# Softcap attention and a bilinear layer on one core: the reciprocals' DMAs from GpSimd, the raw weights requested earlier

## The chip, the cores and the metric

One core of a Trainium2 chip runs the whole program. The metric is the device time of one launch in microseconds (us), lower is better. The engines are TensorE (PE), VectorE (DVE), ScalarE (ACT), GpSimd (POOL) and SyncE (SP). Each works through its own queue of instructions in a fixed order; a DMA is an instruction in the queue of the engine that issues it.

## What is computed

```python
scores = q @ k.T / sqrt(64)                   # 4 batches, 12 heads, 448 tokens, head size 64
scores = 30 * tanh(scores / 30)
attn   = exp(scores - max) / (sum(exp(scores - max)) + 1e-09)
x      = attn @ v                             # joined over heads: 1792 tokens x 768
out    = ((x @ w_a) * (x @ w_b)) @ w_out      # 768 -> 1536 -> 768
```

The inputs q, k, v are fp32, the three weights fp64 (two 32-bit words for each number).

## The kernel before

**Attention.** The 48 heads are taken as 24 pairs, `pi` = 0 to 23; pairs 0 to 11 are batches 0 and 1 (group 0), the others group 1. For a pair, `load_pair` issues nine loads (ldk, ldq, ldv) on SyncE; `prep_pair` transposes k and q on VectorE (tk, tq); `scores` makes psc on TensorE, tanh and exp on ScalarE (L224, L225), and the sum of the probabilities over the key chunks on VectorE (L229, L232, L233). One step later `attend` multiplies by v (pv) and `normalize` ends the pair: 16 small matmuls give the sums of the denominators, VectorE takes the reciprocal `rec` (L268), and because the reciprocals lie along the wrong axis they go through DRAM: `rd[pi]` is written (L269), then read back twice, each time spread over 64 partitions of `den` (L273, two transfers). VectorE multiplies pv by den (L274). For group 0 VectorE rounds the product to `xhi` (L283) and GpSimd makes the rest `xlo` (L284); for group 1 the product is stored in DRAM and read back later. In group 1 pv holds one of the two PSUM buffers of psc until L274.

**The bilinear layer.** `ffn(g)` runs over 12 slices `f` of the hidden size: products with w_a and w_b in three passes of split fp32 (L377 to L379), their product split again, and after every third slice the products with w_out (L408 to L410). It is a generator whose matmuls are laid between the steps of the attention of the next group; what is left of group 0 and all of group 1 comes at the end.

**The weights.** The units are a, b, o of each slice, 36 in all, in the order of use. `load64` requests a raw fp64 unit of 768 KB on SyncE into one of two buffers. `ready_w` makes fp32 of it: two ScalarE passes (L337, L338), three on VectorE (L339 to L341; L341 is the last to read the raw buffer), one addition on GpSimd (L342), and a store `wd` for group 1's use on SyncE (L343). `split_w` makes the high and low part (L359, L360; the low part of a and b on GpSimd) and calls `ready_w` for units up to four ahead. `ready_w` is called first after the steps of `pi` = 8 and begins by requesting raw units up to the one after its own.

**What sets the order.** The steps of a pair follow the letters of `order` (P prep, A attend, S and T scores, N normalize, F a stretch of the layer). That is only the order of the program text: when the kernel is built, a planner simulates the engines with its own cost estimates and writes each engine's queue, an instruction going in when the planner believes its inputs ready, and text order deciding between those that are ready. `tc.keep_in_program_order` pins the first five raw loads behind the instruction of SyncE that stands before them in the text.

Of the kernel before, what the change touches and what calls it, by code (L numbers as in the profile page):

```python
# [117 lines left out]
def kernel(  # L118
# [11 lines left out]
    nc = tc.nc  # L130
    B, H, S, D = q.shape
    NT, DM = out.shape
    DFF = w_a.shape[1]
    P = 128
# [11 lines left out]
    NPG = NPAIR // NG  # L146
    NW = 3 * NF
# [3 lines left out]
    Q = 32  # L151
    AHEAD = 4
# [6 lines left out]
    rd = [dr.tile([2 * NCH, CP], F32, tag=f"rd{i}", name=f"rd{i}") for i in range(NPAIR)]  # L159
# [17 lines left out]
    def f32(ap):  # L177
        return ap.bitcast(F32)
# [10 lines left out]
    raw, stk, prob, pvs = {}, {}, {}, {}  # L189
# [60 lines left out]
    def normalize(pi):  # L250
        del raw["v", pi], stk[pi]
        g, r = divmod(pi, NPG)
        bh, hp = divmod(r, NP)
        t, ts = pvs.pop(pi)
        if ts is None:
            ts = ps_1.tile([P, 512], F32, tag="ps1", name=f"sum_{pi}")
        for m in range(2):
            for i in range(4):
                j, c = divmod(2 * i + m, NCH)
                nc.tensor.matmul(  # L260
                    ts[i * Q : (i + 1) * Q, :CP],
                    sel[:, m],
                    psum[pi % 2][:, j, c * CP : (c + 1) * CP],
                    start=(m == 0),
                    stop=(m == 1),
                )
        rec = sm.tile([P, CP], F32, tag="rec", name=f"rec_{pi}")
        nc.vector.reciprocal(rec, ts[:, :CP])  # L268
        nc.sync.dma_start(rd[pi], rec[0 : P : Q // 2])  # L269
        den = sm.tile([P, S], F32, tag="den", name=f"den_{pi}")  # L270
        for j, o in enumerate(own):
            row = rd[pi][j * NCH : (j + 1) * NCH].rearrange("(o c) p -> o (c p)", o=1)
            nc.sync.dma_start(den[o], row.to_broadcast([D, S]))  # L273
        nc.vector.tensor_mul(den, t[:, :S], den)  # L274
        if g == 0:
            split_x(r, den, nc.gpsimd)
        else:
            nc.sync.dma_start(xd[r], den)

    def split_x(r, xt, eng):  # L280
        bh, hp = divmod(r, NP)
        cs = slice(bh * S, (bh + 1) * S)
        nc.vector.tensor_copy(xhi[:, hp, cs], xt)  # L283
        eng.tensor_sub(xlo[:, hp, cs], xt, f32(xhi[:, hp, cs]))  # L284
# [13 lines left out]
    pos = {"raw": 0, "conv": 0, "split": 0}  # L298

    def load64():  # L300
        t = pos["raw"]
        if t >= NW:
            return
        pos["raw"] += 1
        nm, f, _ = seq[t]
        cs = slice(f * P, (f + 1) * P)
        w = {"a": w_a, "b": w_b, "o": w_out}[nm].bitcast(I32)
        rt = wp.tile([P, DM, 2], I32, tag="w64", name=f"w64{nm}_{f}", bufs=2)
        if nm == "o":
            ld64 = nc.sync.dma_start(rt.rearrange("p n t -> p (n t)"), w[cs, :])  # L310
        else:
            ld64 = nc.sync.dma_start(
                rt.rearrange("p (k f) t -> p k (f t)", k=NK),
                w.rearrange("(k p) f -> p k f", p=P)[:, :, 2 * f * P : 2 * (f + 1) * P],
            )
        if t < AHEAD + 1:
            tc.keep_in_program_order(ld64)
        wraw[t] = rt

    def ready_w():  # L320
        t = pos["conv"]
        if t >= len(seq):
            return
        pos["conv"] += 1
        nm, f, g = seq[t]
        if g:
            wt = wp.tile([P, DM], F32, tag="wt", name=f"wr{nm}_{f}", bufs=AHEAD)
            nc.sync.dma_start(wt, wd[nm, f])
            wfull[t] = wt
            return  # L330
        while pos["raw"] < min(t + 2, NW):
            load64()
        rt = wraw.pop(t)
        hw, lw = rt[:, :, 1], rt[:, :, 0]
        lr = wp.tile([P, DM], I32, tag="wr", name=f"wl{nm}_{f}", bufs=1)
        wt = wp.tile([P, DM], I32, tag="wt", name=f"wt{nm}_{f}", bufs=AHEAD)
        nc.scalar.activation(lr, lw.bitcast(U32), AF.Copy, scale=2.0**-29)  # L337
        nc.scalar.activation(f32(wt), f32(hw), AF.Abs)  # L338
        nc.vector.tensor_scalar_max(f32(wt), f32(wt), TINY_HI)  # L339
        nc.vector.tensor_scalar(wt, wt, 3, 0x3FFFFFFF, op0=ALU.logical_shift_left, op1=ALU.bitwise_and)  # L340
        nc.vector.scalar_tensor_tensor(wt, hw, -0x40000000, wt, op0=ALU.bitwise_and, op1=ALU.bitwise_or)  # L341
        nc.gpsimd.tensor_tensor(wt, wt, lr, op=ALU.add)  # L342
        nc.sync.dma_start(wd[nm, f], f32(wt))  # L343
        wfull[t] = f32(wt)

    def split_w():
        t = pos["split"]
        if t >= len(seq):
            return
        pos["split"] += 1  # L350
        nm, f, g = seq[t]
        wt = wfull.pop(t)
        tag, bufs = ("o", GF) if nm == "o" else ("ab", 3)
        hi = wp.tile([P, DM], F32R, tag=f"wh{tag}", name=f"wh{nm}_{g}_{f}", bufs=bufs)
        lo = wp.tile([P, DM], F32R, tag=f"wl{tag}", name=f"wl{nm}_{g}_{f}", bufs=bufs)
        if g and nm == "b":
            nc.vector.tensor_copy(hi, wt)
        else:
            nc.scalar.copy(hi, wt)  # L359
        (nc.vector if nm == "o" else nc.gpsimd).tensor_sub(lo, wt, f32(hi))  # L360
        wspl[nm, g, f] = (hi, lo)
        while pos["conv"] < min(t + AHEAD, len(seq)):
            ready_w()
# [57 lines left out]
    with ExitStack():  # L421
        load_pair(0)
        nc.sync.dma_start(capt[:, 3:4], cap.rearrange("(a b) -> a b", b=1).to_broadcast([P, 1]))
        make_identity(nc, ident)
        load_pair(1)
        nc.vector.memset(sel, 0.0)
        for m in range(2):
            nc.vector.memset(sel[:, m, m * Q // 2 : (m + 1) * Q // 2], 1.0)
        nc.vector.tensor_scalar_mul(capt[:, 4:5], capt[:, 3:4], -1.0)
        nc.vector.tensor_max(capt[:, 5:6], capt[:, 3:4], capt[:, 4:5])  # L430
        nc.vector.tensor_scalar(bounded, capt[:, 5:6], CAP_MAX, None, op0=ALU.is_le)
        nc.vector.tensor_scalar_min(capt[:, 0:1], capt[:, 5:6], CAP_MAX)
        nc.vector.reciprocal(capt[:, 6:7], capt[:, 0:1])
        nc.vector.tensor_scalar_mul(capt[:, 1:2], capt[:, 6:7], 1.0 / math.sqrt(D))
        nc.scalar.activation(capt[:, 7:8], capt[:, 0:1], AF.Exp, scale=-1.0)
        nc.vector.tensor_scalar_mul(capt[:, 2:3], capt[:, 7:8], 1e-9 / R)

        gen, done, p0 = None, 0.0, 0
        total = NF * 72 * S + NTI * 2 * NF * 3 * HALF

        def run_ffn(upto):
            nonlocal gen, done
            while gen is not None and done < upto:
                try:
                    done += next(gen)
                except StopIteration:
                    gen = None

        prep_pair(0)
        for pi in range(NPAIR + 1):  # L450
            order = "PASNFTF" if pi <= NPG else "SFANPFTF"
            slices = 0
            for step in order:
                if step == "P" and pi + 1 < NPAIR:
                    prep_pair(pi + 1)
                elif step == "A" and pi > 0:
                    attend(pi - 1)
                elif step == "N" and pi > 0:
                    normalize(pi - 1)
                elif step == "S" and pi < NPAIR:  # L460
                    scores(pi, 0)
                    if pi + 2 < NPG - 1:
                        load_pair(pi + 2)
                elif step == "T" and pi < NPAIR:
                    scores(pi, 1)
                elif step == "F":
                    slices += 1
                    run_ffn(total * (pi - p0 + slices / order.count("F")) / (NPG + STRETCH))
            if NPG - AHEAD <= pi < NPG:
                ready_w()  # L470
            if pi == NPG - 1:
                for _ in range(3):
                    split_w()
            if NPG - 1 <= pi + 2 < NPAIR:
                load_pair(pi + 2)
            if pi and pi % NPG == 0:
                run_ffn(1e18)
                gen, done, p0 = ffn(pi // NPG - 1), 0.0, pi + 1
        run_ffn(1e18)
# [37 lines left out]
```

## Time and profile before

| | us |
|---|---|
| median of 3 runs (782.0 to 782.84) | 782.74 |
| the profiled execution | 784.88 |
| its span, first to last instruction | 783.1 |
| TensorE busy | 732.6 (94%) |
| VectorE, ScalarE, GpSimd busy | 424.1, 331.6, 185.4 |
| mean granted clock of TensorE | 0.978 |

The profiled execution is 2.1 us longer than the median, and 1.8 us of it lie outside its span. "Busy" of TensorE counts a matmul that waits inside its pipeline as well. DMA-issuing instructions do not count as busy on any engine; they show as SPq (SyncE's queue) in the timeline. All DMAs of the program stand in SyncE's queue.

### The profile page before, as it was taken

The numbers are of one execution on the slowest core, as the hardware profiler recorded it, in microseconds if no ns is written. First come the engines' busy times: TensorE is split into PE (matmuls) and PEld (weight loads), VectorE is DVE, ScalarE is ACT, GpSimd is POOL, SyncE is SP. The second block draws the span as 40 slices with busy tenths as digits, with TensorE's granted clock in tenths as the row PEclk, the third lists the DMA queues.
The fourth block names the chain that finished last, engine by engine and source line by source line (L and its number), as shares of the span: only waits on it lengthen the run. The fifth ranks groups of instructions, "written<-read, shape, count | busy, mean of one in ns | idle before, by whom it ended". The sixth has DMA issues, their size and how long they took to land.

```text
span 783.1 us, 10042 instructions
## 1 busy us (share of the span) xinstructions
PE 732.6 (94%) x3888; PEld 560.7 (72%) x3888; DVE 424.1 (54%) x562; ACT 331.6 (42%) x402; POOL 185.4 (24%) x102
## 2 busy tenths in 40 slices
PE   5699776997899999998999999999999999999996
PEld 1233223675587677775777787999999999999996
DVE  4576789898624876465665654733213342243222
ACT  5588587575655755354651631022232202212110
POOL 0011244364302343025340221002102201200100
PEclk9899989999899999999899999999999999999999
DMA  6455687885643664336442133542102102111002
GB/s 122 92 105 114 164 180 203 243 228 185 192 120 120 184 198 136 96 108 195 143 156 85 41 105 109 184 135 81 41 21 100 41 21 81 62 41 41 1 35 111
DMA packets 151926, 90.47 MB, mean 116 GB/s; under 512 B 114624, under 2 KB 139456, under 8 KB 151872
## 3 DMA queue, kind: packets, MB, share of 16 engines
q1 hardware_dynamic: 151872, 89.77, 40.3%
q8 instruction: 32, 0.52, 0.3%
q14 instruction: 22, 0.18, 0.1%
HBM read 67.24 MB, written 22.50 MB: 115 GB/s over the span
## 4 chain that ended last, share of the span: by engine, by line
PE 61%; DMA 17%; DVE 11%; issue 4%; SPq 3%; ACT 3%; POOL 1%; DVEq 0%; ACTq 0%; POOLq 0%
PE po L408 6%; PE po L410 6%; PE po L409 6%; PE phb L377 6%; PE phb L378 6%; PE phb L379 6%; PE pha L377 6%; PE pha L379 6%; PE pha L378 6%; DMA den<-rd 5%; PE psc L223 4%; DMA rd<-rec 4%; PE pv L245 2%; DMA xl<-xd 2%; DMA w64o<-in_moe_w_out_dram 2%
## 5 line engine op out<-in xcount | busy, mean ns | idle before, releaser
L223 PE MATMUL psc<-tq,tk 64*128 64x448 f32 (+1 forms) x384 | 97.1, 602 | 25.9 <-DVE den L274 12.3
L408 PE MATMUL po<-who,gh 128*128 128x384 f32 x336 | 114.1, 340 | 1.0 <-DVE acc L414 0.8
L409 PE MATMUL po<-wlo,gh 128*128 128x384 f32 x336 | 112.5, 335 | 0.0
L410 PE MATMUL po<-who,gl 128*128 128x384 f32 x336 | 112.5, 335 | 0.0
L377 PE MATMUL phb<-xhi,whb 128*128 128x448 f32 x288 | 108.0, 375 | 0.0
L377 PE MATMUL pha<-xhi,wha 128*128 128x448 f32 x288 | 107.6, 374 | 0.0
L378 PE MATMUL phb<-xlo,whb 128*128 128x448 f32 x288 | 106.9, 371 | 0.0
L379 PE MATMUL phb<-xhi,wlb 128*128 128x448 f32 x288 | 106.6, 370 | 0.0
L379 PE MATMUL pha<-xhi,wla 128*128 128x448 f32 x288 | 106.2, 369 | 0.0
L378 PE MATMUL pha<-xlo,wha 128*128 128x448 f32 x288 | 106.1, 369 | 0.0
L224 ACT ACTIVATE pf<-psc,capt 128x896 f32<-128x896 f32 x96 | 85.1, 909 | 44.3 <-PE psc L223 43.6
L223 PEld LDWEIGHTS psc<-tq,tk 64*128 64x128 f32 (+1 forms) x384 | 29.5, 180 | 68.6 <-issue 35.4
L225 ACT ACTIVATE pf<-pf,capt 128x1792 f32<-128x1792 f32 (+1 forms) x48 | 77.0, 1604 | 1.2
L414 DVE TENSOR_TENSOR acc<-po,acc 128x384 f32<-128x384 f32 x84 | 45.9, 554 | 48.2 <-PE po L410 48.1
L408 PEld LDWEIGHTS po<-who,gh 128*128 128x128 f32 x336 | 63.0, 188 | 8.5 <-issue 3.2
L384 DVE TENSOR_TENSOR asb<-phb,asb 128x448 f32<-128x448 f32 x48 | 29.8, 621 | 68.7 <-PE phb L379 68.6
L245 PE MATMUL pv<-pf,ldv 128*64 128x448 f32 x288 | 63.6, 563 | 2.5 <-ACT pf L225 2.5
L409 PEld LDWEIGHTS po<-wlo,gh 128*128 128x128 f32 x336 | 63.1, 188 | 0.8 <-issue 0.7
L410 PEld LDWEIGHTS po<-who,gl 128*128 128x128 f32 x336 | 63.0, 188 | 0.7 <-issue 0.7
L377 PEld LDWEIGHTS phb<-xhi,whb 128*128 128x128 f32 x288 | 55.0, 191 | 11.9 <-issue 6.1
L377 PEld LDWEIGHTS pha<-xhi,wha 128*128 128x128 f32 x288 | 54.5, 189 | 11.7 <-issue 6.1
L386 DVE TENSOR_TENSOR gl<-asb,gh 128x448 fp32r<-128x448 f32 x48 | 51.0, 1063 | 21.6 <-ACT gh L385 21.4
(73 smaller groups left out, 971.0 us busy)
## 6 DMA issues: line engine op xcount, KB each, us to landing
w64a<-in_moe_w_a_dram SPq DMA_DIRECT2D x12, 768.0 KB
w64b<-in_moe_w_b_dram SPq DMA_DIRECT2D x12, 768.0 KB
w64o<-in_moe_w_out_dram SPq DMA_DIRECT2D x12, 768.0 KB
ldk<-in_k_dram SPq DMA_DIRECT2D x96, 56.0 KB
ldq<-in_q_dram SPq DMA_DIRECT2D x96, 56.0 KB
ldv<-in_v_dram SPq DMA_DIRECT2D x24, 224.0 KB
den<-rd SPq DMA_DIRECT2D x48, 112.0 KB
out_dram<-acc SPq DMA_DIRECT2D x13, 384.0 KB
```

Of the source, the lines that this page charges most:

```text
L223: nc.tensor.matmul(to, tk[o, at : at + (P if n == 2 else R)], tq[o], start=True, stop=True)
L224: nc.scalar.activation(pf[:, 2 * i : 2 * i + n], psc[:, :n, :S], AF.Tanh, scale=capt[:, 1:2])
L225: nc.scalar.activation(pf, pf, AF.Exp, scale=capt[:, 0:1])
L245: nc.tensor.matmul(t[j * D : (j + 1) * D, :S], tv[:, j * (NC3 + 1) + c], p, start=(c == 0), stop=False)
L377: nc.tensor.matmul(t[:, :S], wh[:, kk], xhi[:, kk, cs], start=(kk == 0), stop=False)
L378: nc.tensor.matmul(t[:, :S], wh[:, kk], xlo[:, kk, cs], start=False, stop=False)
L379: nc.tensor.matmul(t[:, :S], wl[:, kk], xhi[:, kk, cs], start=False, stop=(kk == NK - 1))
L386: nc.vector.tensor_sub(gl[:, cs], asb[h], f32(gh[:, cs]))
L408: nc.tensor.matmul(t[:, :HALF], gh[:, cs], wh, start=(f == fs[0]), stop=False)
L409: nc.tensor.matmul(t[:, :HALF], gh[:, cs], wl, start=False, stop=False)
L410: nc.tensor.matmul(t[:, :HALF], gl[:, cs], wh, start=False, stop=(f == fs[-1]))
L414: nc.vector.tensor_add(acc[:, ti, hs], t[:, :HALF], acc[:, ti, hs])
```

## The change

The write of `rd` and the two reads into `den` are issued by GpSimd instead of SyncE. The first two raw weight units are requested after the steps of `pi` = 6 instead of inside the first `ready_w` (after `pi` = 8), and each `ready_w` requests the unit two ahead at its own end, behind its store, instead of leaving it to the start of the next `ready_w`. Buffers stay as they are: two raw ones.

```diff
         rec = sm.tile([P, CP], F32, tag="rec", name=f"rec_{pi}")
         nc.vector.reciprocal(rec, ts[:, :CP])
-        nc.sync.dma_start(rd[pi], rec[0 : P : Q // 2])
+        nc.gpsimd.dma_start(rd[pi], rec[0 : P : Q // 2])
         den = sm.tile([P, S], F32, tag="den", name=f"den_{pi}")
         for j, o in enumerate(own):
             row = rd[pi][j * NCH : (j + 1) * NCH].rearrange("(o c) p -> o (c p)", o=1)
-            nc.sync.dma_start(den[o], row.to_broadcast([D, S]))
+            nc.gpsimd.dma_start(den[o], row.to_broadcast([D, S]))
...
-        while pos["raw"] < min(t + 2, NW):
+        while pos["raw"] < min(t + 1, NW):
             load64()
...
         nc.sync.dma_start(wd[nm, f], f32(wt))
         wfull[t] = f32(wt)
+        while pos["raw"] < min(t + 3, NW):
+            load64()
...
+            if pi == NPG - AHEAD - 2:
+                for _ in range(2):
+                    load64()
             if NPG - AHEAD <= pi < NPG:
                 ready_w()
```

## Rows read from the trace of the kernel before

**Rows 1.** The page's first lines: span, and busy time of each engine.

```profile
span 783.1 us, 10042 instructions
PE 732.6 (94%) x3888; PEld 560.7 (72%) x3888; DVE 424.1 (54%) x562; ACT 331.6 (42%) x402; POOL 185.4 (24%) x102
```

**Rows 2.** Busy time of each engine in stretches of 20 us, 100 to 160.

```profile
100.00:120.00 20.00, 16.02 (x72) 4.20 (x68) 18.72 (x20) 14.82 (x17) 11.56 (x6) 0.83 0.77 182
120.00:140.00 20.00, 15.09 (x88) 7.60 (x88) 19.27 (x25) 16.51 (x17) 8.44 (x5) 0.91 0.79 217
140.00:160.00 20.00, 19.58 (x107) 14.19 (x107) 17.39 (x20) 11.04 (x15) 10.10 (x6) 1.00 0.80 242
```

**Rows 3.** Timeline of one pair's loop, 45 to 58, and the sixth reciprocal later.

```profile
45.63 0.85 DVE L268 RECIPROCAL rec<-sum 128x112 f32<-128x112 f32 x1
48.23 1.10 SPq L273 DMA_DIRECT2D den<-rd  x2
50.03 1.79 ACT L225 ACTIVATE pf<-pf,capt 128x1792 f32<-128x1792 f32 x1
52.29 0.62 DVE L274 TENSOR_TENSOR den<-pv,den 128x448 f32<-128x448 f32 x1 [2.19 <-DMA den<-rd]
53.26 1.08 DVE L229 TENSOR_TENSOR psum<-pf 128x896 f32<-128x896 f32 x1
53.42 1.93 POOL L284 TENSOR_TENSOR xlo<-den,xhi 128x448 fp32r<-128x448 f32 x1 [8.66 <-DVE xhi L283]
57.56 1.79 ACT L225 ACTIVATE pf<-pf,capt 128x1792 f32<-128x1792 f32 x1
...
95.95 0.85 DVE L268 RECIPROCAL rec<-sum 128x112 f32<-128x112 f32 x1
```

**Rows 4.** The chain that ended last: start, us, what (three of its pieces).

```profile
46.50 1.65 DMA rd<-rec
48.75 3.42 DMA den<-rd
...
216.04 6.10 DMA rd<-rec
```

**Rows 5.** Timeline of the first pair's reciprocal and what it holds up, 20 to 38.

```profile
20.44 0.86 DVE L268 RECIPROCAL rec<-sum 128x112 f32<-128x112 f32 x1 [0.71 <-PE sum L260]
25.22 0.71 SPq L269 DMA_DIRECT2D rd<-rec  x1
31.13 0.62 DVE L274 TENSOR_TENSOR den<-pv,den 128x448 f32<-128x448 f32 x1 [7.69 <-DMA den<-rd]
37.23 0.64 ACT L224 ACTIVATE pf<-psc,capt 128x448 f32<-128x448 f32 x1 [7.73 <-PE psc L223]
```

**Rows 6.** Timeline of the first raw weights, 91 to 136.

```profile
91.40 0.58 SPq L312 DMA_DIRECT2D w64a<-in_moe_w_a_dram  x1
96.89 0.89 ACT L337 ACTIVATE wla<-w64a 128x768 int32<-128x768 uint32 x1 [5.26 <-DMA w64a<-in_moe_w_a_dram]
99.51 1.38 PE L223 MATMUL psc<-tq,tk 64*128 64x448 f32 x4 [4.38 <-ACT pf L224]
105.45 0.96 DVE L341 SCALAR_TENSOR_TENSOR wtb<-w64b,wtb 128x768 int32<-128x768 int32 x1
117.82 0.53 SPq L312 DMA_DIRECT2D w64b<-in_moe_w_b_dram  x1
135.06 0.93 ACT L337 ACTIVATE wlo<-w64o 128x768 int32<-128x768 uint32 x1 [3.31 <-DMA w64o<-in_moe_w_out_dram]
```

**Rows 7.** Waits of SyncE's queue: us in total, times, longest.

```profile
SPq L310 <- DVE wta L341: 32.1, 9, 6.9
SPq L273 <- DMA rd<-rec: 21.0, 12, 4.8
```

**Rows 8.** Who waited for the multiplication by den (L274): us, times.

```profile
  PE psc L223: 12.3, 5
```

**Rows 9.** Timeline of TensorE at 198, the longest of these five waits.

```profile
198.66 1.76 PE L223 MATMUL psc<-tq,tk 64*64 64x448 f32 x4 [7.79 <-DVE den L274]
```

## The prediction

> **What bounds the kernel now.** I began with the page's busy times. TensorE is busy for 732.6 of the 783.1 us [rows 1], so at most some 50 us lie in its visible gaps; but in the attention of group 0 a "busy" TensorE is fed by other engines, so the cadence of the pairs counts there as well. The stretches of 20 us show where: between 100 and 140 TensorE is busy for 16.02 and 15.09 of 20 while VectorE is at 18.72 and 19.27; from 140 it is at 19.58, and what comes later is mostly a full TensorE [rows 2]. What is gained or lost before 140 therefore moves the rest of the program as a whole.
>
> Next came the chain of waits. Between 46 and 94 it runs in each pair through rd (1.65 us) and den (3.42 us), two DMAs one behind the other [rows 4]. The timeline of one pair shows why: VectorE stands 2.19 us before the multiplication by den, and only then come L229 and the next reciprocal [rows 3]. So the reciprocal of one pair waits for the den of the pair before: the round trip is a loop. From the reciprocal at 45.63 to the one at 95.95 are six pairs, 50.32/6 = 8.39 us each. ScalarE alone would need less: its long exp recurs after 57.56 - 50.03 = 7.53 us [rows 3]. VectorE's order, den ahead of L229, is the planner's, who took den to land about 2 us sooner than it did.
>
> Then SyncE, the queue from which things are taken. It stands 21.0 us waiting for rd to land, and 32.1 us at raw loads whose buffer L341 hasn't yet let go [rows 7].
>
> **The change, part by part.**
>
> *First pair.* The reciprocal is ready at 20.44 + 0.86 = 21.30, but rd is issued at 25.22, since pair loads stand ahead of it in SyncE's queue; den is used at 31.13, and ScalarE then has waited 7.73 us [rows 5]. GpSimd has nothing to do there, so 3.92 us of queueing go. Against that stands what a GpSimd DMA costs more, called x for the round trip of a pair.
>
> *The price x.* No row shows a DMA on GpSimd. From below x is 0: same bytes, same engines, issued as on SyncE (two den issues take 1.10, 0.55 each [rows 3]). From above each of the three issues is as long as GpSimd's tensor instruction of 1.93 [rows 3]: 3 x (1.93 - 0.55) = 4.1 us. I take 1.5, nearer to SyncE's issue, the same kind of instruction. The Trainium skill (DMA: Bandwidth & Descriptors, Specifications) gives a first-byte latency of about 1 us on GpSimd's path and 0.6 on SyncE's, so by it an estimate of x would be 2 x 0.4 = 0.8 for two legs; no run here shows it. With 1.5 the first pair gains 3.92 - 1.5 = 2.4 (bounds 0 and 3.9).
>
> *The cadence of the six pairs.* If the planner's estimate of den grows by something like x, den is no longer ready for it when L229 is (exp ends at 50.03 + 1.79 = 51.82, den was used at 52.29 [rows 3]). Then it lays L229, and with it the reciprocal, ahead of den. The loop opens, since a reciprocal then has a whole pair of time for its round trip, and ScalarE's 7.53 is left as the bound: at most 6 x (8.39 - 7.53) = 5.2 us. I take 4. The other bound is that the order stays and each pair pays x: up to 6 x 4.1 = 25 us of loss, 9 us at x = 1.5.
>
> *Requests at pi = 6.* The first raw unit is requested at 91.40; ScalarE stands 5.26 us for it at 96.89 and TensorE 4.38 us at 99.51 [rows 6]. Two pairs earlier is 2 x 8.39 = 16.8 us earlier. But the conversion has no fixed place: the planner lays L337 where it believes the unit landed, and here it was 5.26 us too optimistic. With an earlier request L337 can move forward with it, and the error along with it. So I take half of 4.38, 2.2 us (bounds 0 and 4.4). The unit of 117.82, whose buffer was free at 105.45 + 0.96 = 106.4, and the one that ScalarE awaits for 3.31 us at 135.06 [rows 6] come earlier too; there TensorE is in the bilinear layer with 19.58 of 20 soon after [rows 2], so I count 0 (bounds 0 and 3.3). From the sixth unit on nothing moves: SyncE already stands at the load until L341 frees the buffer [rows 7], and there are still two buffers. The new place of the loads is behind the store L343, which waits for GpSimd's addition: a new wait in SyncE's queue, with the next pair loads behind it. While GpSimd is on time it costs nothing.
>
> *GpSimd's queue.* This is the price of the move. Between 100 and 160 GpSimd works 11.56 + 8.44 + 10.10 = 30.1 of 60 us [rows 2]. Five pairs get their reciprocals about there, each with three issues and a wait for rd to land, in which the queue stands: with x spread over the issues 3 x (0.55 + 0.5) + 1.65 = 4.8 us, 24 in all, into 29.9 that are free. It fits, but additions (L342) and low parts (L360) stand behind it, then ScalarE, whose L337 needs the buffer that L342 frees, and SyncE's store. VectorE being the fuller engine there, I take a loss of 2.5 (bounds 0 and 24).
>
> *Group 1.* psc waited five times for L274, 12.3 us in all, 7.79 of it at 198.66 [rows 8, 9]. Two effects cross. rd took 6.10 us at 216 [rows 4] against 1.65, and a raw load had gone out on the same queue just before; on another queue it need not wait for that. The Trainium skill (DMA: Bandwidth & Descriptors, Queues, rings and completion order) has each DMA engine go round between the queues that have work, packet by packet; by it the 4.45 us of that case would go; the row fits but doesn't show it. Against this, x is added wherever the round trip is exposed, 12 x 1.5 = 18 us if everywhere, and the planner can lay matmuls of the layer into it. I take 0 (bounds 12.3 gained and 18 lost).
>
> *Sum.* -2.4 - 4 - 2.2 + 2.5 + 0 = -6.1 us. On the profiled execution that is 784.88 - 6.1 = 778.8; the median shown lies 2.1 us below that execution, so 782.74 - 6.1 = **776.6, say 777 us**.
>
> **The rivals.**
>
> *A, the loop opens (forecast):* 770 to 781 us, as above.
>
> *B, den stays ahead of L229 (slower).* If the planner prices a GpSimd DMA no longer than SyncE's, VectorE's order stays and six pairs pay x each, +9 us at 1.5, instead of -4: 782.74 - 2.4 - 2.2 + 2.5 + 9 = 789.6, about 790 us. It decides from 6x > 2.1 + 1.6, x of 0.6 us. For it: the 2.19 us by which the planner was short already. Against it: only some 0.5 us separates exp's end from den's use, and den comes from farther.
>
> *C, GpSimd's queue becomes the bound between 100 and 160 (slower).* If half of the 24 us for which rd and den hold GpSimd comes through to VectorE and ScalarE, it is +12 in place of no more than 2.5: 782.74 - 8.6 + 12 = 786 us. For it: half of that stretch is busy already. Against: 29.9 us are free.
>
> *D, it does nothing.* The stall at 96.89 travels with the conversion, den is still in time where it was, and what SyncE is spared had cover: 781.2 to 784.3, about 782.5 us. The Trainium skill (DMA: Bandwidth & Descriptors, Issuing engines are not separate DMA queues) says that all issuers share the same 16 DMA engines, so that spreading saves only the issuer's time. By that rule D is the case; the first pair, 3.9 us late in SyncE's queue [rows 5], is issuer's time and speaks against "nothing".
>
> **How the numbers follow.** Chances: A 0.45, B 0.22, C 0.13, D 0.20. The measurement tells 0.2%, some 1.6 us, from no change. Faster: nearly all of A and a fifth of D, 0.48. Same: most of D and a little of C, 0.16. Slower: B, most of C, a little of A and D, 0.36. A range that leaves out 2 in 10 runs from 769, just under A's own (B's tail with x near 4 and the best of group 1 stay outside), to 791, which takes in B at 1.5 and C. A's own range is 770 to 781.
>
> **What would show it.** In the timeline after: rd on POOL at about 21.3, and ScalarE's wait of 7.73 shortened by some 2.4; L229 and L268 ahead of L274 on VectorE and the pairs at about 7.5 us instead of 8.39 (right), or the old order with 9 to 10 us (B). The time from the end of L268 to L274 gives x. w64a requested near 75, and ScalarE's wait before the first L337 half of 5.26 or less. GpSimd's wait before den, and additions late behind it, would show C. What would make the prediction wrong is x above 2 with den left on the loop, or the conversions late behind GpSimd's DMAs.

## The result, and the profile after

The changed kernel is slower: median 786.26 us (20 runs, 781.4 to 789.1) against 781.88 for the kernel before on the same chip (20 runs, 777.58 to 785.09). The ratio is 1.0056, with a 95% interval of 1.004 to 1.0071. That lies in the predicted range of 769 to 791, but on the other side of no change than the forecast of 777; by its number it is nearest to rival C (786), then to rival B (790), and the traces and runs have to tell which of them it was.

The profiled execution of the changed kernel took 785.17 us, with a span of 783.4. The one of the kernel before took 784.88, which is 3.0 us above the median of its 20 runs. So the two traces end only 0.3 us apart [rows 1], and the loss has to be read from the places inside them, not from their ends.

The page's first lines, after: span, busy time, share and instructions of each engine.

```profile
span 783.4 us, 10095 instructions
...
PE 738.6 (94%) x3888; PEld 559.0 (71%) x3888; DVE 417.4 (53%) x562; ACT 332.2 (42%) x402; POOL 223.8 (29%) x174
```

GpSimd has 174 instructions instead of 102: the 72 moved DMAs. The timeline below shows them as POOL rows.

Timeline of the kernel after: start, length, engine (SPq and POOL for DMA issues), line, operation; in brackets the wait before it.

```profile
21.62 0.72 POOL L269 DMA_DIRECT2D rd<-rec  x1 [20.30 <-DVE rec L268]
24.41 1.38 DVE L232 SCALAR_TENSOR_TENSOR psum<-pf,capt,psum 64x448 f32<-64x448 f32 x2 [0.94 <-ACT pf L225]
30.27 0.62 DVE L274 TENSOR_TENSOR den<-pv,den 128x448 f32<-128x448 f32 x1 [4.49 <-DMA den<-rd]
33.12 0.85 DVE L268 RECIPROCAL rec<-sum 128x112 f32<-128x112 f32 x1
...
53.26 0.85 DVE L268 RECIPROCAL rec<-sum 128x112 f32<-128x112 f32 x1
56.88 1.04 POOL L273 DMA_DIRECT2D den<-rd  x2 [1.92 <-DMA rd<-rec]
61.13 0.62 DVE L274 TENSOR_TENSOR den<-pv,den 128x448 f32<-128x448 f32 x1 [3.62 <-DMA den<-rd]
62.10 1.08 DVE L229 TENSOR_TENSOR psum<-pf 128x896 f32<-128x896 f32 x1
63.10 0.85 DVE L268 RECIPROCAL rec<-sum 128x112 f32<-128x112 f32 x1
...
69.02 0.83 SPq L312 DMA_DIRECT2D w64a<-in_moe_w_a_dram  x1
72.73 0.85 DVE L268 RECIPROCAL rec<-sum 128x112 f32<-128x112 f32 x1
75.27 0.91 ACT L337 ACTIVATE wla<-w64a 128x768 int32<-128x768 uint32 x1 [3.05 <-DMA w64a<-in_moe_w_a_dram]
79.09 1.17 POOL L273 DMA_DIRECT2D den<-rd  x2 [4.65 <-DMA rd<-rec]
87.66 0.84 DVE L268 RECIPROCAL rec<-sum 128x112 f32<-128x112 f32 x1
96.68 0.85 DVE L268 RECIPROCAL rec<-sum 128x112 f32<-128x112 f32 x1
...
107.55 0.62 DVE L274 TENSOR_TENSOR den<-pv,den 128x448 f32<-128x448 f32 x1
```

- Up to the reciprocal at 87.66 the loop is closed as before [rows 3]: L274, then L229, then the next reciprocal. The reciprocal at 96.68 is the first that stands ahead of the multiplication by den of the pair before it (107.55), and so it goes on to the end of group 0. In the pairs around 53 VectorE now stands 3.62 us for den where it stood 2.19.
- From the end of the reciprocal to the start of L274 it takes 61.13 - 54.11 = 7.02 us here; before it took 52.29 - 46.48 = 5.81 [rows 3]. Over three pairs of each trace (reciprocals at 43.00, 53.26 and 63.10; 45.63, 54.26 and 62.43 before) the means are 7.09 (6.82 to 7.44) and 5.53 (5.35 to 5.81): x = 1.56.
- The reciprocals at 43.00 and 72.73 are three pairs apart, 9.91 us each. Before, the same three pairs (45.63 to 70.69) took 8.35 each. The difference is 1.56, the whole of x.
- The next pair takes 87.66 - 72.73 = 14.93: it holds the first conversion and an rd that lands late, 4.65 us after GpSimd stands waiting for it, beside the raw loads that were requested at 69.02.
- The ninth reciprocal (pi = 8) is at 113.68, 17.7 us later than the 95.95 of [rows 3]. Pair 12 is late by 10.8 (161.52 for 150.75) and pair 13 by 1.2 (192.07 for 190.83), but a pair's lateness isn't TensorE's: the planner laid other numbers of layer matmuls between the pairs.

So I counted TensorE's matmuls up to 140, by line: operation and count, busy time and mean ns of one, idle time before them. First the kernel after, whose list holds no product with w_a or w_b:

```profile
L223 PE MATMUL psc<-tq,tk 64*128 64x448 f32 (+1 forms) x200 | 54.7, 654 | 11.4 <-DVE tq L210 7.2 <-ACT pf L224 4.2
```

The kernel before, same view and stretch:

```profile
L223 PE MATMUL psc<-tq,tk 64*128 64x448 f32 (+1 forms) x216 | 55.0, 610 | 13.6 <-DVE tq L210 7.4 <-ACT pf L224 6.2
...
L377 PE MATMUL pha<-xhi,wha 128*128 128x448 f32 x6 | 3.0, 505 | 0.0
L378 PE MATMUL pha<-xlo,wha 128*128 128x448 f32 x5 | 2.5, 496 | 0.0
L379 PE MATMUL pha<-xhi,wla 128*128 128x448 f32 x5 | 2.5, 490 | 0.0
```

After, 16 score matmuls are missing and 16 of the layer, with four of pv 36 in all (the short ones of the sums left out). The times of the three layer lines can't be added: a matmul is recorded as some 0.5 us long, and the next one starts before it ends. The first window below has 309 matmuls in 60.00 us, 0.19 us each; at that pace, an estimate, TensorE is some 7 us behind at 140. Then the windows of 140 to 200 (stretch, length, busy time of PE, PEld, DVE, ACT and POOL with instructions, granted clock, DMA share, GB/s), after:

```profile
140.00:200.00 60.00, 60.00 (x309) 40.22 (x308) 42.57 (x53) 35.33 (x42) 29.82 (x25) 1.00 0.62 171
```

and before:

```profile
140.00:200.00 60.00, 51.78 (x269) 37.54 (x267) 50.65 (x53) 36.22 (x46) 30.45 (x16) 0.96 0.72 220
```

After, TensorE has no gap there; before, it has 8.2 us of gaps, most of them the wait of 7.79 for L274, that of pair 13, which ends at 198.66 [rows 9]. The same count says where it stands: 52 matmuls behind at 190 (600 for 652), 12 behind at 200 (647 for 659), 16 ahead at 400 (1592 for 1576), and by the end 0.3 us behind. The stop of the kernel before at 198.66 gives back most of what was lost ahead of it. So the loss at the end can't be followed from 140 through these two traces, of which one is 3.0 us above its median. The medians differ by 4.4.

### The profile page after: what moved, and what is told of

Same layout as the page of the kernel before. It is cut to its first block, busy times and chain, and to the rows that moved or that the text cites. A ratio compares the mean times of both kernels' runs of the same rounds, so it can differ in the third digit from the quotient of the medians.

```text
span 783.4 us, 10095 instructions
## 1 busy us (share of the span) xinstructions
PE 738.6 (94%) x3888; PEld 559.0 (71%) x3888; DVE 417.4 (53%) x562; ACT 332.2 (42%) x402; POOL 223.8 (29%) x174
## 4 chain that ended last, share of the span: by engine, by line
PE 62%; DVE 2%; issue 2%; POOL 2%; DMA 1%; ACT 1%; DVEq 0%; POOLq 0%; ACTq 0%
PE po L410 7%; PE po L412 7%; PE po L411 7%; PE pha L379 6%; PE pha L380 6%; PE pha L381 6%; PE phb L379 6%; PE phb L380 6%; PE phb L381 6%; PE psc L223 3%; PE pv L245 2%; DMA den<-rd 1%; PE pv L247 1%; POOL wto L342 1%; POOL wlb L362 1%
## 5 line engine op out<-in xcount | busy, mean ns | idle before, releaser
L223 PE MATMUL psc<-tq,tk 64*128 64x448 f32 (+1 forms) x384 | 100.8, 621 | 14.4 <-DVE tq L210 7.2
L245 PE MATMUL pv<-pf,ldv 128*64 128x448 f32 x288 | 68.1, 588 | 7.7 <-ACT pf L225 5.0
L362 POOL TENSOR_TENSOR wlb<-wrb,whb 128x768 fp32r<-128x768 f32 x12 | 22.2, 1849 | 149.5 <-PE pha L381 140.6
```

The source lines that it names most:

```text
L223: nc.tensor.matmul(to, tk[o, at : at + (P if n == 2 else R)], tq[o], start=True, stop=True)
L245: nc.tensor.matmul(t[j * D : (j + 1) * D, :S], tv[:, j * (NC3 + 1) + c], p, start=(c == 0), stop=False)
```

## The experiments

Two theories stood at the start. In the first (Loop), the loss is x on the closed loop of group 0, and the change would have gained if VectorE's order had opened. In the second, GpSimd's queue (rival C) or the earlier requests cost what is lost. Every ratio is to the kernel before, run in the same rounds on the same chip.

**The two halves alone.** First rd and den on GpSimd, raw requests as before:

```diff
-        nc.sync.dma_start(rd[pi], rec[0 : P : Q // 2])
+        nc.gpsimd.dma_start(rd[pi], rec[0 : P : Q // 2])
...
-            nc.sync.dma_start(den[o], row.to_broadcast([D, S]))
+            nc.gpsimd.dma_start(den[o], row.to_broadcast([D, S]))
```

> Only rd and den on GpSimd, raw weights requested as before. Theory Loop (the round trip through DRAM is 1.5 us longer on GpSimd's queue and stands in the loop of VectorE's order, seven pairs between 33 and 96): pairs at 9.8 us instead of 8.4, some 10 us lost there, 3 to 4 won at the first pair, so slower by about 6 us, ratio 1.006 to 1.009. Theory Requests (the raw units requested at pi = 6 run into the round trips between 69 and 84 and are the loss): ratio 0.998 to 1.002. GpSimd's queue as the cause between 84 and 108 (den 6 us late behind an addition) would show here as well: den issued late behind L342.

Measured: 1.005 (1.0028 to 1.0072), 787.58 us. Timeline of this kernel, one pair's loop and the next reciprocal:

```profile
62.10 0.62 DVE L274 TENSOR_TENSOR den<-pv,den 128x448 f32<-128x448 f32 x1 [3.70 <-DMA den<-rd]
63.06 1.09 DVE L229 TENSOR_TENSOR psum<-pf 128x896 f32<-128x896 f32 x1
64.07 0.85 DVE L268 RECIPROCAL rec<-sum 128x112 f32<-128x112 f32 x1
...
73.93 0.85 DVE L268 RECIPROCAL rec<-sum 128x112 f32<-128x112 f32 x1
```

The order stands, this pair takes 9.86 us (64.07 to 73.93), and the loss is that of the whole change. This trace, 4.0 us longer in its span than that of the kernel before, lets the loss be followed by the same count: TensorE is 30 matmuls behind at 96, 50 at 190, 9 at 200, after the stop of the kernel before, and 27 at 220. So more than half of what is lost up to 190 is lost by 96, ahead of the stretch of rival C; what part GpSimd's queue has in the rest isn't shown. Then the raw requests alone, rd and den on SyncE:

```diff
-        while pos["raw"] < min(t + 2, NW):
+        while pos["raw"] < min(t + 1, NW):
...
+        while pos["raw"] < min(t + 3, NW):
+            load64()
...
+            if pi == NPG - AHEAD - 2:
+                for _ in range(2):
+                    load64()
```

> Only the raw weights requested earlier, rd and den on SyncE as before. Theory Loop: faster by 1 to 3 us, ratio 0.996 to 0.999, ScalarE's wait before the first L337 3 us instead of 5.3. Theory Requests: slower, ratio 1.003 to 1.006, with a round trip of 8 us or more for the pair whose rd goes out at about 74, behind the two raw units.

Measured: 0.999 (0.9963 to 1.0017), 782.9 us. Timeline of this kernel, the first unit:

```profile
76.09 0.58 SPq L312 DMA_DIRECT2D w64a<-in_moe_w_a_dram  x1
81.31 0.89 ACT L337 ACTIVATE wla<-w64a 128x768 int32<-128x768 uint32 x1 [5.30 <-DMA w64a<-in_moe_w_a_dram]
```

The request is 15.3 us earlier than in [rows 6], and ScalarE waits 5.30 us for it where it waited 5.26: the planner moved the conversion forward with the request, and the stall travelled along. This half on its own makes no difference that the interval shows, and the loss is there with the first alone.

**Which pairs lose.** rd and den on GpSimd for group 0 only, then for group 1 only:

```diff
-            nc.sync.dma_start(den[o], row.to_broadcast([D, S]))
+            (nc.gpsimd if pi < NPG else nc.sync).dma_start(den[o], row.to_broadcast([D, S]))
```

(the same for rd; `pi >= NPG` in the second)

> rd and den on GpSimd for pairs 0 to 11 alone, on SyncE for the others; requests as before, loop not opened. Theory Loop: nearly the whole loss of the move is here, ratio 1.003 to 1.007. If the longer round trip costs in group 1, where psc waits for the multiplication by den: 0.999 to 1.002.

> rd and den on GpSimd for pairs 12 to 23 alone. Theory Loop: TensorE has matmuls of the layer to fill the round trip, ratio 0.998 to 1.002. If group 1 pays 1.5 us for each of 12 pairs: 1.01 to 1.02 at the full price, 1.003 to 1.007 where a part is covered.

Measured: 1.0063 (1.004 to 1.0086), 787.77 us, for group 0; 0.9998 (0.9974 to 1.0022), 783.88 us, for group 1. The loss is group 0's. In group 1 TensorE waits less for L274, as the line on who waited for it shows (us, times), but the time doesn't follow:

```profile
  PE psc L223: 4.1, 6
```

It was 12.3 us in five waits [rows 8].

**The loop opened by hand.** The multiplication by den of one pair is laid behind the reciprocal of the next, on top of the changed kernel:

```diff
         nc.vector.reciprocal(rec, ts[:, :CP])
+        for late in tails:
+            late()
+        tails.clear()
...
+        if pi < NPG - 1:
+            def tail():
+                tc.keep_in_program_order(nc.vector.tensor_mul(den, t[:, :S], den))
+                split_x(r, den, nc.gpsimd)
+            tails.append(tail)
+            return
         nc.vector.tensor_mul(den, t[:, :S], den)
```

> The changed kernel with the loop opened by hand: for pairs 0 to 10 the multiplication by den is pinned behind the next pair's reciprocal. Theory Loop: the pairs between 33 and 72 recur at ScalarE's 7.5 us instead of 9.8, some 10 us less than the changed kernel, ratio to the kernel before 0.990 to 0.996. If what is lost before 140 isn't what decides the end, it stays at 1.003 to 1.007.

Measured: 0.9928 (0.9899 to 0.9956), 777.3 us. Reciprocals follow each other by 7.5 to 9.2 us up to 61.09. The same edit on the kernel before, with rd and den on SyncE:

> The kernel before with the loop opened by hand in the same way, nothing else. Theory Loop: six pairs at 7.5 instead of 8.4 us, 5 us less, ratio 0.992 to 0.996. If time lost before 140 is made up later by TensorE's filler, ratio 0.998 to 1.002.

Measured: 1.0001 (0.9979 to 1.0023), 782.49 us, which is not what Loop expected, but the other value put on record, by which time lost before 140 is made up later anyway. Timeline of this kernel (L270 is the reciprocal, L274 rd, L282 the multiplication):

```profile
29.68 0.85 DVE L270 RECIPROCAL rec<-sum 128x112 f32<-128x112 f32 x1
30.94 1.99 SPq L199 DMA_DIRECT2D ldq<-in_q_dram  x4
33.97 0.60 SPq L274 DMA_DIRECT2D rd<-rec  x1
...
40.37 0.62 DVE L282 TENSOR_TENSOR den<-pv,den 128x448 f32<-128x448 f32 x1 [2.30 <-DMA den<-rd]
```

The reciprocal is done at 30.53 but rd is issued at 33.97, behind loads of a later pair in SyncE's queue, and L282 waits again; from 37.22 to 90.69 six pairs take 8.9 us each. So the cadence isn't won, with SyncE's queue as the next wait. But the first pair is: its reciprocal is followed by the next after 9.2 us, 15.9 before, and TensorE is 26 matmuls ahead of the kernel before at 140. At 180 it is 2 behind. In between it stood 2.13 us for xhi at 145.59 and 1.47 us for the multiplication by den at 163.06, and the long stop of [rows 9] is there as well:

```profile
197.73 1.76 PE L223 MATMUL psc<-tq,tk 64*64 64x448 f32 x4 [6.30 <-DVE den L287]
```

(L287 is the multiplication by den of the pairs that weren't opened.) The crossing case is the move and the open order without the earlier requests:

> rd and den on GpSimd and the loop opened by hand, raw weights requested as before. If the queue and the opened loop together make the gain and the earlier requests add nothing (alone they were at 0.999): ratio 0.991 to 0.995. If the requests are worth something once the loop is open: 0.995 to 0.999.

Measured: 0.985 (0.982 to 0.988), 772.09 us, by its ratio the fastest of all, and it beats both kernels. The timeline, and what L282 waited for (us, times):

```profile
30.01 0.85 DVE L270 RECIPROCAL rec<-sum 128x112 f32<-128x112 f32 x1
31.15 0.57 POOL L274 DMA_DIRECT2D rd<-rec  x1 [5.26 <-DVE rec L270]
...
60.97 0.85 DVE L270 RECIPROCAL rec<-sum 128x112 f32<-128x112 f32 x1
61.74 0.56 DVE L282 TENSOR_TENSOR den<-pv,den 128x448 f32<-128x448 f32 x1
...
76.45 0.84 DVE L270 RECIPROCAL rec<-sum 128x112 f32<-128x112 f32 x1
...
190.49 1.02 PE L223 MATMUL psc<-tq,tk 64*128 64x448 f32 x4 [1.21 <-DVE den L287]
```

```profile
  DMA den<-rd: 0.8, 2
```

rd goes out 0.29 us behind the reciprocal; L282 stands behind L270 and waits 0.8 us in all; six pairs take (76.45 - 30.01)/6 = 7.74 us, close to ScalarE's 7.53 [rows 3]. GpSimd issues the same 72 DMAs as in the changed kernel. So as long as the order is open its queue isn't the bound, and this part of the second theory falls. The way to the end is longer than the loop, though: this kernel is 30 matmuls ahead of the kernel before at 140, hardly more than the 26 of the one with SyncE, still 25 ahead at 180, and 57 at 200, since TensorE's stop for the multiplication by den of pair 13 is 1.21 us here (190.49) and not 7.79. Why the lead is kept from 140 to 180 in the one and not in the other isn't shown.

**Group 1 with the loop open.** The changed kernel opened, and the kernel of 772.09 us, each with group 1's rd and den back on SyncE (the edit of group 0 only above):

> The changed kernel with the opened loop, but group 1's rd and den back on SyncE. If GpSimd's DMAs cost in group 1, faster than the opened changed kernel (0.9928): 0.988 to 0.991. If group 1 is indifferent to the queue: 0.991 to 0.995.

> The opened loop with rd and den on GpSimd for pairs 0 to 11, on SyncE for 12 to 23, raw weights as before. Group 1 was indifferent to the queue without the opened loop (0.9998): 0.983 to 0.988 if it still is; below 0.983 if GpSimd's DMAs cost there, above 0.988 if GpSimd's queue helps there.

Measured: 0.991 (0.9878 to 0.9942), 775.66 us, and 0.9865 (0.983 to 0.9899), 771.58 us. Neither can be told from its partner with group 1 on GpSimd (0.9928 and 0.985).

**What the earlier requests cost there.** They are all that lies between 0.9928 and 0.985. Each half was put on the kernel of 772.09 us alone. First the two units after `pi` = 6, with the rest as before:

```diff
+            if pi == NPG - AHEAD - 2:
+                for _ in range(2):
+                    load64()
```

> The opened loop with rd and den on GpSimd (0.985 without any earlier request), and of the earlier requests only the first two units after pi = 6. If the conversions that come with these two stretch pairs 6 and 7 from 7.5 us to 11 or more before there is anything to do with the weights: 0.990 to 0.995. If the other half of the edit (the unit two ahead, behind the store) is what costs: 0.984 to 0.988.

Then each further unit behind the store, the first two inside the first `ready_w`:

```diff
         wfull[t] = f32(wt)
+        while pos["raw"] < min(t + 3, NW):
+            load64()
```

> The opened loop with rd and den on GpSimd, and of the earlier requests only the second half: each conversion requests the unit two ahead at its end, the first two units stay at pi = 8. If the first two cost: 0.983 to 0.988, pairs 6 and 7 at 7.5 us. If this half costs: 0.990 to 0.995.

Measured: 0.9951 (0.9927 to 0.9975), 778.84 us, and 0.9932 (0.9906 to 0.9958), 776.79 us. Either half costs about what both do. Timeline of the first of these (L350 is ScalarE's first pass):

```profile
61.06 0.85 DVE L270 RECIPROCAL rec<-sum 128x112 f32<-128x112 f32 x1
65.44 0.92 ACT L350 ACTIVATE wla<-w64a 128x768 int32<-128x768 uint32 x1 [1.82 <-DMA w64a<-in_moe_w_a_dram]
74.44 0.84 DVE L270 RECIPROCAL rec<-sum 128x112 f32<-128x112 f32 x1
85.48 0.85 DVE L270 RECIPROCAL rec<-sum 128x112 f32<-128x112 f32 x1
```

The conversions come 16.7 us earlier than in the kernel of 772.09 us (65.44 for 82.16), and fall into pairs that ScalarE paces: these two take 13.4 and 11.0 us where they took 7.9 and 7.6. Pair 12 has its reciprocal at 145.11 instead of 142.99, so nothing of the conversions' 16.7 us is won. Timelines of the second, and of the kernel of 772.09 us, for the fourth and fifth raw unit:

```profile
94.45 2.24 SPq L325 DMA_DIRECT2D w64b<-in_moe_w_b_dram  x1
...
106.82 0.38 SPq L323 DMA_DIRECT2D w64o<-in_moe_w_out_dram  x1
```

```profile
90.48 0.59 SPq L325 DMA_DIRECT2D w64b<-in_moe_w_b_dram  x1
...
102.45 0.35 SPq L323 DMA_DIRECT2D w64o<-in_moe_w_out_dram  x1
```

In the program text the request is "one unit more ahead"; in the queue these two go out 4.0 and 4.4 us later (the first unit of all 1.9), each directly behind a store, and the store waits for GpSimd's addition.

Neither is where the time goes, though. By the count of matmuls both are level with the kernel of 772.09 us at 180 (634 and 631 for 630), and at 200 both are 28 behind (688 for 716). In between lies TensorE's stop for pair 13, 1.21 us in that kernel; of the first of the two:

```profile
190.58 1.75 PE L223 MATMUL psc<-tq,tk 64*64 64x448 f32 x4 [5.21 <-DVE den L287]
```

In the second it is 5.91 us, at 192.35. The multiplication ends no later in the first than in the kernel of 772.09 us (189.81 is its start in both); TensorE had fewer matmuls to do before it. After the stop four score matmuls take 1.75 us, 1.02 in that kernel, and the granted clock of 180 to 200 is 0.83 in both, against 1.00: part of the stretch ran at the lower of the two levels, 1.2 GHz. With both halves together, the kernel of 0.9928, it is otherwise: the stop is 1.05 us, and TensorE is 26 matmuls behind as early as 96, where the pairs stretched by conversions lie.

## Why the prediction was wrong

**The step that failed** is the cadence of the six pairs: "then it lays L229, and with it the reciprocal, ahead of den". The order on VectorE stayed, and the pairs up to 72.73 paid x, 1.56 us each. That is rival B, which had a chance of 0.22 against 0.45; that the time fell on rival C's 786 is chance, since the pairs of group 0 take 1.56 us more from 43 on, and with the order open the same DMAs on GpSimd cost nothing. The condition I gave for B, x above 0.6 (strictly 0.75, as the first pair's gain falls with x too: 7x > 3.62 + 1.6), was met by the x of 1.5 that I had taken myself: with x so large, only the planner's reaction stood between a gain of 4 and a loss of 9, and no row showed that reaction. The order did open from the reciprocal at 96.68 on, but there the conversions pace the pairs. Why the planner kept the order before can only be argued: VectorE's wait before L274 grew from 2.19 to 3.62 us, by 1.43, nearly all of x, which is what would be seen if the planner prices a GpSimd DMA like one of SyncE. That the open order turns the loss into a gain, in the presence of the move, is shown: 1.005 against 0.985 with nothing else changed in the text, though the planner laid the rest anew too.

**The price x** was right: 1.5 taken, 1.56 measured. The estimate from the first-byte figures of the Trainium skill (DMA: Bandwidth & Descriptors, Specifications), 0.8 for two legs, is half of what the trace shows; the measurement decides.

**The first pair** came out near in its number, and by luck: 2.4 us predicted, and the second reciprocal is at 33.12 instead of 36.33, 3.2 us earlier. rd goes out at 21.62 instead of 25.22 [rows 5], but from there to L274 it takes 8.65 us instead of 5.91, so den is used only 0.86 us earlier (30.27 for 31.13). More than half of the rest (1.36 of 2.35 us) comes from VectorE's order, of which I had expected nothing there: L232 now lies ahead of L274 (24.41), where it stood behind it. Before:

```profile
31.67 1.36 DVE L232 SCALAR_TENSOR_TENSOR psum<-pf,capt,psum 64x448 f32<-64x448 f32 x2
```

**The size of B.** It was priced at 790, and 786.3 was measured, because I had taken all that is lost before 140 to move the rest of the program as a whole. That step is wrong as well: TensorE is 52 matmuls (some 10 us) behind at 190 and 12 at 200, since the stop of 7.79 us of the kernel before [rows 9] is no longer there, as I read it because late work of the layer fills it; and the lead of 26 matmuls that the open order on SyncE had at 140 was gone by 180. The move of group 1's DMAs is the smaller part of that: between 140 and 200 TensorE is busy for 57.58 us with group 0 alone on GpSimd, and for 53.67 with group 1 alone.

**The requests** were predicted at -2.2 and are worth nothing alone (0.999): what rival D said of them, the stall that travels. With the loop open they cost 0.985 to 0.9928, some 6 us. I had counted the place behind the store as free "while GpSimd is on time"; the queue shows requests up to 4.4 us later, but TensorE is none the worse for it at 180. The cost comes at the stop for pair 13 where one half is in, and before 96 where both are.

**GpSimd's queue**, +2.5 predicted, shows its delays; whether they have a price while the order is closed isn't shown. Timeline of the kernel after, one late den, and a case of group 1 with a raw load ahead of it (at 215.60 on SyncE):

```profile
90.68 0.56 POOL L269 DMA_DIRECT2D rd<-rec  x1
96.91 1.82 POOL L342 TENSOR_TENSOR wta<-wta,wla 128x768 int32<-128x768 int32 x1 [3.82 <-DVE wta L341]
98.66 1.07 POOL L273 DMA_DIRECT2D den<-rd  x2
...
218.19 0.56 POOL L269 DMA_DIRECT2D rd<-rec  x1
223.64 1.05 POOL L273 DMA_DIRECT2D den<-rd  x2 [4.89 <-DMA rd<-rec]
```

den goes out 8 us behind rd, since an addition that waits for L341 stands between them; L274, at 107.55, doesn't wait for it, being laid behind the next reciprocal by then.

**Group 1**, 0 predicted, 0.9998 measured: right. But one of its two effects is hardly there. rd at 218.19 takes 5.45 us to the issue of den, against the 6.10 of [rows 4] on SyncE's queue, so its own queue gave back 0.65 of the 4.45 us that I had worked out. The Trainium skill (DMA: Bandwidth & Descriptors, Queues, rings and completion order) has the DMA engines go round between the queues, packet by packet. No run here shows the packets; by the rows, a small write near 768 KB loads stays slow on a queue of its own too.

**Left open.** Why the planner kept its order; and how what happens up to 140 becomes what is left at the end. Each variant is planned anew, and how many matmuls lie ahead of TensorE's stop for pair 13 moves the time by as much as the change does: a shorter stop there gave back most of what the changed kernel had lost, and about half of the lead of the kernel of 772.09 us at 200 came with it (32 matmuls of 57). No run held that layout fixed.

## What to carry to other kernels

Before a DMA is moved to another engine's queue, look where its consumer stands in its own engine's queue: if the consumer stands ahead of the work that starts the next round trip, what the new way costs more is paid in each round, here 1.56 us. A move and a change of order can each be worth nothing or less alone and 1.5% together, so try the pair. An earlier request won nothing here, since the work that uses the data moved forward with it; look in the queue, not in the program text, for when it goes out. And what is won or lost early need not be there at the end: count the work done at several places, and look for the stop that takes it up.

## What was not expected of the hardware

An rd of 3.5 KB needed nearly as long near raw loads on another queue as on the same one (5.45 us and 6.10): GpSimd stood 4.65 us for it at 79.09 and 4.89 us at 223.64, where it stood 1.92 us at 56.88 with no raw load near it. And a round trip of two DMAs from GpSimd took 7.09 us where SyncE's took 5.53; 1.0 of the difference in the pair shown lies between the end of the reciprocal and the issue of den (54.11 to 56.88, against 46.48 to 48.23 [rows 3]).
